# Normalizing k into zero-padded blocks, g into q, and w_out by column halves in a fused attention and feed-forward kernel

## The chip, the cores and the metric

The kernel runs on one core of a Trainium2 chip. A core has TensorE (PE, matrix products into PSUM; the profile lists its weight loads apart as PEld), VectorE (DVE), ScalarE (ACT), GpSimd (POOL) and SyncE (SP, which here only issues DMAs); 16 DMA engines move data between HBM and the on-chip memory SBUF, or inside SBUF. Each engine works its own instructions in order and waits on semaphores. The metric is the device time in microseconds (us) of one execution.

## What is computed

Attention over q, k, v of shape (8 batches, 12 heads, 448 positions, 64), with q and k RMS-normalized, followed by a feed-forward layer over 3584 rows of width 768 with 2048 hidden units and a hard-swish:

```python
def rmsnorm(x, g):
    rms = np.sqrt(np.mean(x * x, axis=-1, keepdims=True) + 1e-06)
    return x / rms * g
q_n, k_n = (rmsnorm(q, g_q), rmsnorm(k, g_k))
scores = (1.0 / np.sqrt(64)) * np.matmul(q_n, k_n.transpose(0, 1, 3, 2))
attn = softmax(scores)                  # exp(s - max) / sum
out = np.matmul(attn, v)                # heads side by side: x, 3584 x 768
h = x @ w_in
g = h * np.clip(h + 3.0, 0.0, 6.0) / 6.0
return (g @ w_out).astype(np.float32)
```

All inputs and the output are float32; the products run in bfloat16 and add up in float32.

## The kernel before

The work is cut into 48 pairs of heads (6 pairs a batch). A pair's 448 positions lie as three full blocks of 128 and a rest of 64; the rests of the two heads share one block. Two pairs make a group, and a group's q, k and v come by SP's DMAs into rings of three buffers (`q_st`, `k_st`, `v_st`; `load_q`, `load_k`, `load_v`, lines 248 to 275). For a pair p:

- `square` (line 306) on POOL, DVE or ACT, `stats_sum` (L315, a DVE reduce) and `stats_rstd` (L322, L325 on ACT) give 1/rms of every row. From group 8 on (`NFAST`) squares and normalizes are only on POOL.
- `normalize` (L330) writes k times 1/rms and q times 1/rms, as bfloat16, into `qk_r`, one instruction for k and one for q.
- For pairs 0 to 13 PE transposes the eight 128x128 blocks (`transposes`, L346), and `put_q` and `put_k` copy them from PSUM: q times g' = g_q g_k / 8 into `qT_r`, k into the zero-padded `kpad` (seven blocks; in blocks 0 to 2 only the first head's 64 rows are filled, in 4 to 6 only the second's).
- From pair 14 on (`TD`) one transposing DMA (`transposes_dma`, L352) moves the eight blocks from `qk_r` into `kqT_r`, a view of the weight staging buffers `w_st`; then `scale_k` (L361) multiplies the transposed k by g' into `kpad`, in two halves of 64 partitions, on DVE or POOL. q is read by PE as it was transposed.
- `score` (L375) makes seven products of 448 columns into two PSUM banks, `expo` (L381) takes their exponentials on ACT, `weigh` (L395, L401) multiplies by v with a column of ones, `divide` (L410, L411, DVE) divides, and x is transposed into `xT`, by PE and `put_x` for pairs 0 to 13 (L423, L434), by a DMA after that (L427).

The feed-forward of a batch needs the x of its six pairs: 16 `h` items (L438, six matmuls each), after each a `relu` (L444, ACT) and a `gate` (L449, DVE) that frees the PSUM bank and writes `gT`; then `y` items (L457, 16 matmuls of 384 columns for one block of 128 rows and one half of the columns), a copy to `y_r` (a view of `w_st`, three rows) and a store. `h` and `y` share three banks `m`, and the two score banks when attention is done. The weights come in 16 loads of 768 KB into the three buffers `w_st` (`load_w`, L288) and are cast to bfloat16 by `cast_w` (L278): eight of w_in by columns, eight of w_out by two row blocks each. Every `y` item waits for all eight of w_out.

The order is not written out by hand. `Plan` (line 41) holds every step with a key, dependencies, and for each engine that may do it an assumed duration; it walks through the time that these give, lets each engine take the known step with the smallest key, and choose among engines by when each would be done (POOL's durations count 0.4 of their length in this choice). On PE, `h` and `y` items fill in between attention's steps by a given share. What comes out is one fixed order of instructions on each engine and each DMA queue, so a changed duration in the plan changes orders everywhere.

Of the kernel before, what the change touches and what calls it, by code (L numbers as in the profile page):

```python
# [8 lines left out]
FP32 = mybir.dt.float32  # L9
BF16 = mybir.dt.bfloat16  # L10
# [35 lines left out]
class Plan:  # L46
# [5 lines left out]
    PRICE = {"POOL": 0.4}  # L52
# [104 lines left out]
def kernel(  # L157
# [29 lines left out]
    WR = 2  # L187
    NW = 3
    TD = 14
# [13 lines left out]
    gprime = const.tile([P, 1], FP32, name="gprime")  # L203
    eps_c = const.tile([P, 1], FP32, name="eps_c")
# [5 lines left out]
    kpad = ring(NK, [P, 7 * P], BF16, "kpad")  # L210
# [5 lines left out]
    qT_r = ring(NK, [P, S], BF16, "qT")  # L216
# [3 lines left out]
    t_r = ring(3, [P, S], FP32, "t_sb")  # L220
    w_st = ring(NW, [P, NKT * WC], FP32, "w_st")

    kqT_r = [w_st[i][:, 0:W4].bitcast(BF16).rearrange("p (a c) -> p a c", a=2) for i in range(NK)]
    y_r = [w_st[i][:, W4:W4 + DM] for i in range(3)]
# [55 lines left out]
    def load_w(n):  # L280
        if n < NWI:
            dst = w_st[n % NW][:].rearrange("p (kt f) -> p kt f", f=WC)
            src = moe_w_in[:, n * WC:(n + 1) * WC].rearrange("(kt p) f -> p kt f", p=P)
        else:
            c = (n - NWI) * WR * P
            dst = w_st[n % NW][:].rearrange("p (ft m) -> p ft m", m=DM)
            src = moe_w_out[c:c + WR * P, :].rearrange("(ft p) m -> p ft m", p=P)
        nc.sync.dma_start(out=dst, in_=src)  # L288

    def cast_w(eng, n):  # L290
        if n < NWI:
            out = w_in_sb[:, :, n * WC:(n + 1) * WC]
            in_ = w_st[n % NW][:].rearrange("p (kt f) -> p kt f", f=WC)
        else:
            c = (n - NWI) * WR
            out = w_out_sb[:, c:c + WR, :]
            in_ = w_st[n % NW][:].rearrange("p (ft m) -> p ft m", m=DM)
        copy(eng, out=out, in_=in_)
# [51 lines left out]

    def transposes_dma(p):
        nc.sync.dma_start_transpose(  # L352
            out=kqT_r[p % NK][:].rearrange("p a (t c) -> p (a t) c", t=4),
            in_=qk_r[p % NQ][:].rearrange("p a t h d -> p (a t h d)"),
        )

    def scale_k(eng, p, part):

        kp = kpad[p % NK]
        rows, c0 = ((lo, 0), (hi, NT * P))[part]  # L360
        eng.tensor_scalar_mul(kp[rows, c0:c0 + W4], kqT_r[p % NK][rows, 0, :], gprime[rows])  # L361

    def put_q(eng, p):
        if eng is nc.scalar:
            eng.activation(out=qT_r[p % NK][:], in_=t_ps[:, 1, 0:S], func=COPY, scale=gprime[:])
        else:
            eng.tensor_scalar_mul(qT_r[p % NK][:], t_ps[:, 1, 0:S], gprime[:])
# [6 lines left out]
    def score(p, i, n):  # L374
        nc.tensor.matmul(  # L375
            out=sc_r[n % 2][:, 0:S], lhsT=kpad[p % NK][:, i * P:(i + 1) * P],
            rhs=qT_r[p % NK][:] if p < TD else kqT_r[p % NK][:, 1, 0:S], start=True, stop=True,
        )
# [124 lines left out]

    def make_g():
# [57 lines left out]
    def y_item(b, t, part, place):  # L562
        n, c = YC, part * YC
        deps = [*w_ops[NWI:], *gates[b], *(gates[b - 1] if t == NT else [])]
# [4 lines left out]
        if part == 0:  # L569
            y_parts.append([])  # L570
        k = len(y_parts) - 1
# [4 lines left out]
        y_parts[k].append(it.out)  # L576
        if part == DM // YC - 1:
            stores.append(plan.dma((-1, 0), 1 if t < NT else 2, P * DM * 4,
                                   lambda: y_store(b, t, ys), y_parts[k]))

    def feed_forward(b):

        if b:
            ts = (NT, *range(NT)) if b % 2 == 0 else range(NT)
            ys = [(t, c) for t in ts for c in range(DM // YC)]
            for i, (t, c) in enumerate(ys):
# [5 lines left out]
    gate_ops, y_parts, y_rest = [], [], {}  # L592
    NWI = DFF // WC
    YC, YLAG = 384, 0.12
# [4 lines left out]
    for n in range(len(W_AFTER)):  # L599
        w_loads.append(plan.dma((GP * W_AFTER[n], 3 + n), 1, P * 1536 * 4, lambda n=n: load_w(n),  # L600
                                [at(w_ops, n - NW)], hold=True))
        w_ops.append(add((GP * W_AFTER[n], 9), [("DVE", 1350, lambda n=n: cast_w(V, n)),
# [14 lines left out]
    pad = by((0, 9), 1400, 1400, fill_e, [])  # L617
    squares = []
# [3 lines left out]
    for p in range(NPAIR):  # L622
        g = p // GP
        if p % GP == 0:
# [22 lines left out]
            for j, (p0, n) in enumerate(single):  # L647
                j = min(j, len(todo) - 1)
                for a in range(2):
                    m = len(squares)  # L650
                    s1 = add((p0 - 2, 2), [("POOL", 960 * n, lambda a=a, p0=p0, n=n, m=m: square(G, a, p0, n, m % 2)),
                                           ("DVE", 50 + 650 * n, lambda a=a, p0=p0, n=n, m=m: square(V, a, p0, n, m % 2)),
                                           ("ACT", 190 + 400 * n, lambda a=a, p0=p0, n=n, m=m: square(A_, a, p0, n, m % 2))][:3 if g < NFAST else 1],
# [14 lines left out]
        for a in range(2):  # L668
            nrm.append(add((p - 2, 4), [("POOL", 1070, lambda p=p, a=a: normalize(G, p, a)),
                                        ("DVE", 700, lambda p=p, a=a: normalize(V, p, a))][:2 if g < NFAST else 1],  # L670
                           [rstd_op[a, p], at(tr, p - NQ)]))
# [7 lines left out]
        if p >= TD:  # L679
            old = at(scs, 7 * (p - NK) + 6)  # L680
            tr.append(plan.dma_transpose((p - 1, 3), 4 * P * W4, lambda p=p: transposes_dma(p),
                               [nrm[2 * p], nrm[2 * p + 1], old, *w_ops[-NW:], at(pk, 2 * (p - NK)), at(pk, 2 * (p - NK) + 1)]))
            pq.append(tr[p])
            for part in range(2):
                pk.append(add((p - 1, 1 + part), [("DVE", 250, lambda p=p, part=part: scale_k(V, p, part)),
                                                  ("POOL", 500, lambda p=p, part=part: scale_k(G, p, part))],
                              [tr[p], mg, old]))
# [62 lines left out]
```

## Time and profile before

| | |
|---|---|
| median of 3 runs | 463.37 us (462.51 to 465.12) |
| the profiled execution | 462.64 us, span 460.8 us |
| busy: PE | 427.1 us, 93% |
| busy: DVE, ACT, POOL | 258.7, 292.2, 274.3 us |
| mean clock granted to PE | 0.981 |
| `scale_k` (L361) | POOL 34 of 1.586 us, DVE 34 of 1.108 us |
| `normalize` (L330) on POOL | 45 of k at 1.090 us, 44 of q at 1.092 us |
| transposing DMA of q and k (L352) | 34, median 3.1 us from issue to landing, longest 6.3 |
| moved by DMA | 70.60 MB, mean 153 GB/s |

A row of the groups names a line, an engine, what is written and read, and how often, then total and mean busy time. A row of stretches gives a start and an end, then for each engine the busy time in it. The chain of waits follows the work back from the end: at each step to what released it; its rows have a start, a length and what took it. In the table of 40 slices each digit is a busy share in tenths, and PEclk is the clock that PE was granted.

### The profile page before, as it was taken

To read this page: it belongs to the slowest core of one execution; us is meant where nothing else is said; L and a number is where in the kernel's file an instruction comes from. 1 tells how busy PE (TensorE), PEld (TensorE's weight loads), DVE (VectorE), ACT (ScalarE), POOL (GpSimd) and SP (SyncE) were. 2 spreads that over 40 slices of the span, in tenths; PEclk is the share of its full clock that TensorE was granted. 3 is DMA by queue.
4 is the path that set the end of the run, shared out by engine and by line. 5 is a ranking of instruction groups with operands and counts; after the bars stand their busy time and mean duration, and the time that the engine had idled before them with its cause. 6 is when DMAs were issued, how large, how long until landed. Compare 5 with 4: busy or idle time off the path is not lost.

```text
span 460.8 us, 9210 instructions
## 1 busy us (share of the span) xinstructions
PE 427.1 (93%) x3512; PEld 257.6 (56%) x3512; DVE 258.7 (56%) x420; ACT 292.2 (63%) x601; POOL 274.3 (60%) x249
## 2 busy tenths in 40 slices
PE   0787699699999989999999999999999999999996
PEld 0354466455566645665656656656666655555563
DVE  6689899855756656658565467576444243222300
ACT  3677878786476768768776677766766553333311
POOL 6799879984889779777897769696431000000000
PEclk9978999989999999999999999999999999999999
DMA  4899999992788897786696785934332220001021
GB/s 118 213 296 287 302 274 309 291 297 81 168 189 194 181 178 163 188 205 160 142 199 139 192 166 126 219 92 100 83 68 57 58 49 34 36 36 55 18 98 68
DMA packets 125804, 70.60 MB, mean 153 GB/s; under 512 B 77120, under 2 KB 120128, under 8 KB 125760
## 3 DMA queue, kind: packets, MB, share of 16 engines
q1 hardware_dynamic: 124928, 69.56, 60.0%
q8 instruction: 27, 0.44, 0.4%
q10 hardware_dynamic: 832, 0.46, 0.4%
q14 instruction: 17, 0.14, 0.1%
HBM read 45.61 MB, written 11.01 MB: 123 GB/s over the span
## 4 chain that ended last, share of the span: by engine, by line
PE 78%; DMA 6%; DVE 5%; SPq 5%; POOL 2%; issue 1%; ACT 1%; POOLq 0%; ACTq 0%
PE m L457 26%; PE m L438 25%; PE sc L375 10%; PE av L401 6%; PE sc L457 5%; DMA w_st<-qk 3%; PE sc L438 3%; PE av L395 2%; DMA w_st<-in_moe_w_in_dram 2%; DMA v_st<-in_v_dram 1%; SPq L275 1%; SPq L267 1%; DVE gT L449 1%; POOL qk L330 1%; DVE ssq L315 1%
## 5 line engine op out<-in xcount | busy, mean ns | idle before, releaser
L381 ACT ACTIVATE eT<-sc 128x448 bf16<-128x448 f32 x336 | 174.7, 543 | 66.5 <-PE sc L375 62.4
L438 PE MATMUL m<-xT,w_in_sb 128*128 128x448 bf16 x696 | 161.3, 352 | 4.0 <-DVE gT L449 3.6
L457 PE MATMUL m<-w_out_sb,gT 128*128 128x384 bf16 x768 | 150.1, 326 | 0.0
L457 PEld LDWEIGHTS <-gT 128*128 128x128 bf16 x896 | 87.0, 98 | 61.3
L438 PEld LDWEIGHTS <-w_in_sb 128*128 128x128 bf16 x768 | 74.4, 98 | 72.2 <-issue 6.1
L449 DVE SCALAR_TENSOR_TENSOR gT<-t_sb,m 128x448 bf16<-128x448 f32 x116 | 71.1, 619 | 60.8 <-ACT t_sb L444 59.7
L444 ACT ACTIVATE t_sb<-m,half_c 128x448 f32<-128x448 f32 x116 | 73.1, 633 | 24.0 <-PE m L438 21.9
L375 PE MATMUL sc<-w_st,kpad 128*128 128x448 bf16 x238 | 80.7, 352 | 0.5 <-ACT eT L381 0.5
L361 POOL TENSOR_SCALAR kpad<-w_st,gprime 64x512 bf16<-64x512 bf16 x34 | 53.9, 1586 | 18.8 <-DMA w_st<-qk 18.0
L315 DVE TENSOR_REDUCE ssq<-sq 128x16 f32<-128x1024 f32 (+1 forms) x56 | 58.7, 1060 | 4.4 <-POOL sq L312 2.8
L401 PE MATMUL av<-vaug,eT 128*128 128x65 bf16 x1152 | 56.7, 197 | 0.5 <-ACT eT L381 0.5
L401 PEld LDWEIGHTS <-eT 128*128 128x128 bf16 x1152 | 52.8, 101 | 5.2 <-issue 0.9
L330 POOL TENSOR_TENSOR qk<-k_st,rstd 128x512 bf16<-128x512 f32 x45 | 49.0, 1090 | 4.2 <-ACT rstd L325 3.4
L361 DVE TENSOR_SCALAR kpad<-w_st,gprime 64x512 bf16<-64x512 bf16 x34 | 37.7, 1108 | 20.6 <-DMA w_st<-qk 20.0
L330 POOL TENSOR_TENSOR qk<-q_st,rstd 128x512 bf16<-128x512 f32 x44 | 48.1, 1092 | 1.9 <-ACT rstd L325 1.7
L312 POOL TENSOR_TENSOR sq<-k_st 128x1024 f32<-128x1024 f32 (+1 forms) x24 | 41.9, 1747 | 11.2 <-DMA k_st<-in_k_dram 10.6
L312 POOL TENSOR_TENSOR sq<-q_st 128x1024 f32<-128x1024 f32 (+1 forms) x26 | 44.3, 1703 | 4.3 <-DMA q_st<-in_q_dram 2.6
L375 PEld LDWEIGHTS <-kpad 128*128 128x128 bf16 x336 | 31.2, 99 | 27.0 <-issue 6.2
L395 PE MATMUL av<-vaug,eT 128*128 128x130 bf16 x192 | 43.5, 227 | 0.0
L375 PE MATMUL sc<-qT,kpad 128*128 128x448 bf16 x98 | 35.4, 393 | 7.5 <-ACT eT L381 6.3
L278 POOL CAST vaug<-v_st 128x512 bf16<-128x512 f32 x34 | 21.0, 619 | 35.9 <-PE av L401 34.6
L278 ACT COPY w_st<-m 128x384 f32<-128x384 f32 x32 | 15.2, 476 | 30.3 <-PE m L457 28.0
(59 smaller groups left out, 254.4 us busy)
## 6 DMA issues: line engine op xcount, KB each, us to landing
out_dram<-w_st SPq DMA_DIRECT2D x24, 384.0 KB, 2.9
k_st<-in_k_dram SPq DMA_DIRECT2D x23, 384.0 KB, 4.1
q_st<-in_q_dram SPq DMA_DIRECT2D x23, 384.0 KB, 4.4
v_st<-in_v_dram SPq DMA_DIRECT2D x23, 384.0 KB, 4.5
w_st<-in_moe_w_in_dram SPq DMA_DIRECT2D x8, 768.0 KB, 7.0
w_st<-in_moe_w_out_dram SPq DMA_DIRECT2D x8, 768.0 KB, 6.0
out_dram<-w_st SPq DMA_DIRECT2D x8, 192.0 KB, 2.7
k_st<-in_k_dram SPq DMA_DIRECT2D x46, 32.0 KB, 3.6
```

The source lines that it names most:

```text
L312: eng.tensor_tensor(out=sq, in0=x, in1=x, op=A_MULT)
L315: nc.vector.tensor_reduce(out=ssq_r[(p // GP) % 2][:, a, p % GP:p % GP + n, :].rearrange("p r s -> p (r s)"), in_=sq_r[m][:, 0:n].rearrang ...
L330: eng.tensor_tensor(out=qk_r[p % NQ][:, a].rearrange("p t h d -> p h t d"), in0=raw(a, p, 1).rearrange("p r (h t) d -> p (r h) t d", h=2), ...
L361: eng.tensor_scalar_mul(kp[rows, c0:c0 + W4], kqT_r[p % NK][rows, 0, :], gprime[rows])
L375: nc.tensor.matmul(out=sc_r[n % 2][:, 0:S], lhsT=kpad[p % NK][:, i * P:(i + 1) * P], rhs=qT_r[p % NK][:] if p < TD else kqT_r[p % NK][:, 1 ...
L381: nc.scalar.activation(out=eT_r[n % NE][:, 0:S], in_=sc_r[n % 2][:, 0:S], func=EXP, bias=0.0, scale=1.0,)
L395: nc.tensor.matmul(out=av_ps[:, i, 0:2 * W], lhsT=e[3][:, cols], rhs=va[:, 3].rearrange("p h d -> p (h d)"), start=True, stop=False, skip_ ...
L401: nc.tensor.matmul(out=av_ps[:, i, h * W:(h + 1) * W], lhsT=e[4 * h + t][:, cols], rhs=va[:, t, h], start=False, stop=(t == NT - 1 and h = ...
L438: nc.tensor.matmul(out=m[:, 0:S], lhsT=w_in_sb[:, kt, f * P:(f + 1) * P], rhs=xT[:, kt, b % NX, x_slot(b)], start=(kt == 0), stop=(kt == N ...
L444: nc.scalar.activation(out=t[:], in_=m[:, 0:S], func=RELU, bias=half_c[:], scale=1.0 / 6.0,)
L449: nc.vector.scalar_tensor_tensor(out=gT[:, f, (b % 2) * S:(b % 2 + 1) * S], in0=t[:], scalar=1.0, in1=m[:, 0:S], op0=A_MIN, op1=A_MULT,)
L457: nc.tensor.matmul(out=m[:, 0:n], lhsT=gT[:, f, c0:c0 + P], rhs=w_out_sb[:, f, c:c + n], start=(f == 0), stop=(f == NFT - 1),)
```

## The change

- From pair 14 on `normalize_k` (POOL, one instruction a head) writes the normalized k straight into seven zero-padded blocks in `w_st` (`kq_st`; its zeros are set once by `clear_kq`, after the last weight casts), and `normalize_q` (DVE, eight instructions of 128x64) writes q times 1/rms times g' (`gq_b`, loaded by two broadcasting DMAs) behind them. One DMA transposes the eleven blocks into `kq_r`, of which `kpad` and `qT_r` are now views. `scale_k` is gone.
- w_out is loaded and cast by column halves, four row blocks at a time; a `y` item waits only for its half, and the `y` items of batch 0 are reordered to begin with the first half of two row blocks.
- `y_r` has its own two buffers.
- In the plan POOL's durations count 0.6 instead of 0.4, and the assumed durations of squares, normalizes and casts are others, by which three squares of groups 4 to 7 go to ACT, all weight casts to POOL, and the order of every engine shifts.

```diff
-    PRICE = {"POOL": 0.4}
+    PRICE = {"POOL": 0.6}
...
-    WR = 2
+    WR = 4
...
-    kpad = ring(NK, [P, 7 * P], BF16, "kpad")
+    kq_r = ring(NK, [P, 11 * P], BF16, "kq")
+    kpad = [x[:, 0:7 * P] for x in kq_r]
...
-    qT_r = ring(NK, [P, S], BF16, "qT")
+    qT_r = [x[:, 7 * P:7 * P + S] for x in kq_r]
...
+    y_r = ring(2, [P, DM], FP32, "y_sb")
...
-    kqT_r = [w_st[i][:, 0:W4].bitcast(BF16).rearrange("p (a c) -> p a c", a=2) for i in range(NK)]
-    y_r = [w_st[i][:, W4:W4 + DM] for i in range(3)]
+    KQ = 11 * P // 2
+    kq_st = [w_st[i][:, 0:KQ].bitcast(BF16) for i in range(NQ)]
...
-            c = (n - NWI) * WR
-            out = w_out_sb[:, c:c + WR, :]
+            half, r = divmod(n - NWI, NFT // WR)
+            out = w_out_sb[:, r * WR:(r + 1) * WR, half * YC:(half + 1) * YC]
...
+    def normalize_k(eng, p):
+        blocks = kq_st[p % NQ][:, 0:7 * P]
+        for h in range(2):
+            c0 = h * (NT * P)
+            eng.tensor_tensor(
+                out=blocks[:, c0:c0 + W4].rearrange("p (t c) -> p t c", t=4)[:, :, h * D:(h + 1) * D],
+                in0=raw(0, p, 1)[:, 0, 4 * h:4 * h + 4, :],
+                in1=rstd_r[(p // GP) % 2][:, 0, p % GP, 4 * h:4 * h + 4].unsqueeze(2)
+                .to_broadcast([P, 4, D]), op=A_MULT,
+            )
+
+    def normalize_q(p):
+        x = raw(1, p, 1)
+        out = kq_st[p % NQ][:, 7 * P:11 * P].rearrange("p (t h d) -> p t h d", t=4, h=2)
+        for h in range(2):
+            for t in range(4):
+                nc.vector.scalar_tensor_tensor(
+                    out=out[:, t, h, :], in0=x[:, 0, 4 * h + t, :],
+                    scalar=rstd_r[(p // GP) % 2][:, 1, p % GP, 4 * h + t:4 * h + t + 1],
+                    in1=gq_b[:], op0=A_MULT, op1=A_MULT,
+                )
...
-            out=kqT_r[p % NK][:].rearrange("p a (t c) -> p (a t) c", t=4),
-            in_=qk_r[p % NQ][:].rearrange("p a t h d -> p (a t h d)"),
-        )
-
-    def scale_k(eng, p, part):
-
-        kp = kpad[p % NK]
-        rows, c0 = ((lo, 0), (hi, NT * P))[part]
-        eng.tensor_scalar_mul(kp[rows, c0:c0 + W4], kqT_r[p % NK][rows, 0, :], gprime[rows])
+            out=kq_r[p % NK][:].rearrange("p (t c) -> p t c", c=P), in_=kq_st[p % NQ])
...
+    def clear_kq(eng, i):
+        blocks = kq_st[i][:, 0:7 * P].rearrange("p (t c) -> p t c", c=P)
+        eng.memset(blocks[:, 0:NT, D:P], 0.0)
+        eng.memset(blocks[:, NT + 1:7, 0:D], 0.0)
...
-        deps = [*w_ops[NWI:], *gates[b], *(gates[b - 1] if t == NT else [])]
+        deps = [*w_ops[NWI + part * NFT // WR:NWI + (part + 1) * NFT // WR], *gates[b], *(gates[b - 1] if t == NT else [])]
...
+            if b == 1:
+                ys = [(0, 0), (1, 0), (0, 1), (1, 1), (2, 0), (2, 1)]
...
-        w_ops.append(add((GP * W_AFTER[n], 9), [("DVE", 1350, lambda n=n: cast_w(V, n)),
+        w_ops.append(add((GP * W_AFTER[n], 9), [("DVE", 1500, lambda n=n: cast_w(V, n)),
...
+    ckq = [by((2 * TD, 0), 600, 350, lambda e, i=i: clear_kq(e, i), w_ops[-NW:]) for i in range(NQ)]
+    lgb = plan.dma((GP * 4, 0), 2, P * D * 8, load_gb)
+    mgb = add((GP * 5, 0), [("DVE", 300, make_gb)], [lgb])
...
-                                           ("DVE", 50 + 650 * n, lambda a=a, p0=p0, n=n, m=m: square(V, a, p0, n, m % 2)),
-                                           ("ACT", 190 + 400 * n, lambda a=a, p0=p0, n=n, m=m: square(A_, a, p0, n, m % 2))][:3 if g < NFAST else 1],
+                                           ("DVE", 1350 * n, lambda a=a, p0=p0, n=n, m=m: square(V, a, p0, n, m % 2)),
+                                           ("ACT", 170 + 445 * n, lambda a=a, p0=p0, n=n, m=m: square(A_, a, p0, n, m % 2))][:3 if g < NFAST else 1],
...
-        for a in range(2):
-            nrm.append(add((p - 2, 4), [("POOL", 1070, lambda p=p, a=a: normalize(G, p, a)),
-                                        ("DVE", 700, lambda p=p, a=a: normalize(V, p, a))][:2 if g < NFAST else 1],
-                           [rstd_op[a, p], at(tr, p - NQ)]))
+        if p < TD:
+            for a in range(2):
+                nrm.append(add((p - 2, 4), [("POOL", 1150, lambda p=p, a=a: normalize(G, p, a)),
+                                            ("DVE", 1250, lambda p=p, a=a: normalize(V, p, a))],
+                               [rstd_op[a, p], at(tr, p - NQ)]))
+        else:
+            nrm.append(add((p - 2, 4), [("POOL", 1250, lambda p=p: normalize_k(G, p))],
+                           [rstd_op[0, p], at(tr, p - NQ), ckq[p % NQ]]))
+            nrm.append(add((p - 2, 4), [("DVE", 1400, lambda p=p: normalize_q(p))],
+                           [rstd_op[1, p], at(tr, p - NQ), w_ops[-1], w_ops[-2], w_ops[-3], mgb]))
...
-            for part in range(2):
-                pk.append(add((p - 1, 1 + part), [("DVE", 250, lambda p=p, part=part: scale_k(V, p, part)),
-                                                  ("POOL", 500, lambda p=p, part=part: scale_k(G, p, part))],
-                              [tr[p], mg, old]))
+            pk += [tr[p], tr[p]]
```

## The prediction

> **What bounds the kernel now.** I read the page's first two parts, then the busy time of each engine by stretches that I cut where the PE row changes, then the chain of waits inside the two stretches that lose time, then the rows of the lines that the diff touches.
>
> The page:
>
> ```profile
> span 460.8 us, 9210 instructions
> PE 427.1 (93%) x3512; PEld 257.6 (56%) x3512; DVE 258.7 (56%) x420; ACT 292.2 (63%) x601; POOL 274.3 (60%) x249
> ...
> PEclk9978999989999999999999999999999999999999
> ```
>
> PE is busy for 93% of the span, so no other engine's share matters by itself; what can be won is PE's idle time and the slices in which its clock falls below 9 tenths.
>
> The busy time by stretches (start and end; length; PE, PEld, DVE, ACT, POOL; granted clock, DMA share, GB/s):
>
> ```profile
> 12.00:58.00 46.00, 34.84 (x327) 21.32 (x328) 36.77 (x65) 35.40 (x88) 40.88 (x37) 0.89 1.01 276
> 58.00:84.00 26.00, 25.95 (x256) 16.15 (x255) 24.01 (x45) 21.06 (x46) 22.83 (x19) 1.00 1.01 296
> 84.00:97.00 13.00, 8.39 (x92) 5.39 (x91) 9.05 (x15) 10.05 (x20) 12.94 (x11) 0.74 0.97 252
> 113.00:347.00 234.00, 230.80 (x1978) 140.76 (x1976) 143.19 (x203) 165.08 (x339) 176.75 (x144) 1.00 0.70 158
> 347.00:457.00 110.00, 110.00 (x728) 63.98 (x725) 28.22 (x48) 43.62 (x78) 1.56 (x1) 1.00 0.15 47
> ```
>
> From 58 us on PE is full but for two stretches. In 84 to 97 it is busy 8.39 of 13 us at clock 0.74, which is 6.2 us of work at full clock: 6.8 us lost. In 113 to 347 it idles 3.2 us. The rest of the loss is the start (12 us before the first scores) and 12 to 58, where the DMA engines are full (share 1.01) and the clock is 0.89.
>
> The chain of waits in the first of these stretches (start, us, what):
>
> ```profile
> 84.08 1.90 DVE qk L330
> ...
> 90.80 1.46 ACT w_out_sb L278
> 92.26 0.45 ACT eT L381
> 92.75 0.97 PE sc L375 x2
> ```
>
> Here PE has attention of pairs 10 to 12 alone, no feed-forward matmul of batch 0 being left, and it waits for one DVE normalize (1.90 us, against 0.69 when nothing holds it) and for a w_out cast that ACT does ahead of an exponential. In the second stretch:
>
> ```profile
> 162.28 6.28 DMA w_st<-qk
> 168.56 0.02 issue
> 168.58 0.35 DVE kpad L361
> 168.93 0.03 issue
> 168.96 0.63 DVE gT L449
> ...
> 298.47 3.24 DVE kpad L361
> ```
>
> DVE waits for a transposing DMA to land, because scale_k stands at the head of its queue, and the gate that frees a PSUM bank for PE stands behind it. Three such places (168, 270, 302) hold nearly all of the 3.2 us.
>
> **The change part by part.** The sum is made against this execution: 460.8 us of span and 1.8 around it, 462.64 us. The median of the runs shown, 463.37, lies 0.7 above.
>
> 1. scale_k goes (34 pairs, L361): 34 x 1.586 = 53.9 us of POOL and 34 x 1.108 = 37.7 us of DVE, none of it PE time. With it goes the only DVE instruction of the steady stage that waits for a DMA, so what it made late goes: the 3.2 us of idle PE. What is late next is a gate behind the new normalize_q (3). I take 2.2 us of gain; ends 0 and 3.2.
>
> 2. normalize_k (34 pairs, POOL, two instructions of 128x256 for one of 128x512 at 1.09): ends 1.09 (per column alone) and 1.3 (one POOL memset of little data, 0.1, as fixed cost, twice). 1.2. POOL also loses the q normalize (1.09 a pair). In 113 to 347 it falls from 176.75 to about 176.75 - 52.4 - 36.0 + 3.6 = 92 us of 234, 39%. Cover is not needed.
>
> 3. normalize_q (34 pairs, DVE, eight instructions of 128x64, two SBUF operands). No row shows one. The reduces of 128x1024 (1.212) and 128x512 (0.679) give 1.04 ns a column and 0.146 us fixed, so 64 columns are 0.213, eight are 1.7 us; two gates in a row started 0.53 apart at 0.61 each, so overlap could bring eight to 1.1. Above that comes waiting for POOL: the seven DVE normalizes of 128x512 took 1.27 on average, 0.58 over the free 0.69, while POOL was busy 88%. At 39% that is 0.26 an instruction: 0.3 if one of the eight is caught, 2.1 if all are. I take 1.7 + 1.0 = 2.7; ends 1.1 and 3.8. The transposing DMAs of before are issued from 113.4 to 346.9, 33 intervals of 7.08 us a pair. DVE has 143.2 / 33 = 4.3 us of work a pair, less 1.1, plus 2.7: 5.9 of 7.08, so it is covered by DVE's idle time. A gate behind it can be 2 to 3 us late; I leave 1.0 us of the idle time of (1) standing for that. Without the cover see rival B.
>
> The Trainium skill (SBUF — State Buffer, Who interferes with whom) says that a DVE instruction with two SBUF inputs and a GpSimd instruction that reads SBUF lock each other out whole. The trace agrees: at 51.05 a DVE normalize took 1.53 us, ending 0.54 after the POOL normalize that held it. That rule speaks against moving q from POOL to DVE in eight pieces; were each piece caught by a whole 1.09 us instruction the sum would gain nothing and rival B would hold, with POOL's lower load as its limit.
>
> 4. The transposing DMA takes 11 blocks for 8. Four blocks land in a median 3.0 us and eight in 3.1, so about 3.2; the longest of eight took 6.3. It is issued some 15 us before the pair's first score (162.3 against 177.2 for pair 22), and the scale that followed is gone: nothing on the path, ends 0 and, if a landing of 6.3 met a late issue, 1 us. On the engines: 256-byte packets took 22 ns (113 to 119 us), 34 x 3 x 128 x 22 ns / 16 = 18 us in 234, share 0.70 to 0.78.
>
> 5. w_out by halves and y of batch 0 reordered. In the new order PE starts y of batch 0 inside the weigh of pair 11, after t13, where before it had only h of batch 1, after x11. Between the last h of batch 0 and that point stand 10 scores, one weigh, two transposes of qk and one of xn (4.1 us of PE); before there were 14 scores, two weighs and more. ACT starts exponentials 0.49 apart, so 4.9 us is the floor, and DVE's chain from weigh 10 to t13 (0.9 divide, 1.3 puts, 0.4 x, 1.2 reduce, 0.4 put) with the hops some 5 to 7. So 1 to 3 us lost for 6.8; I take 3.0, a gain of 3.8, ends 0 and 5.8. It needs the four casts of the first half of w_out. All 16 weight casts are now on POOL; adding the mean durations of its rows along POOL's new order, the last cast of the first half stands behind 75 us of POOL work and the last of all behind 86, where before the last one on POOL stood behind 96 and ended at 113. POOL was 12 us behind its own work by 80 us, so 88 and 99; PE should come to y at about 89 to 90. The ACT cast at 90.80 is gone with it.
>
> The w_out packets are 1,536 bytes for 3,072. Packets of 1,024 took 55 ns and of 3,072 141, so 76: 1.5 us more of all engines, under the full PE of 58 to 84. Nothing; without that cover 1.5.
>
> 6. Squares early: three of 128x1024 go from POOL (1.89) to ACT, at about twice the 0.62 of 128x512. ACT loses two casts of 1.46. Nothing on PE in 12 to 58, where the DMA queue order of the first seven groups is nearly unchanged; the first transposes now wait for POOL's k behind a v cast: 0.3 us of loss, ends -2 and +2.
>
> 7. SP: two loads of gq_b, gk_b (under 1 us each) pass ahead of a k load at full PE: nothing, at most 1. The transpose of pair 15 stands ahead of that of 14, then a store that waits for the second half of y, then the k and q of group 10, which was loaded at 90 and will be at about 115. Pair 20 is scored near 160: 30 us of slack over a 15 us chain. Six POOL memsets (0.2 to 0.4) and normalize_q of 14 wait for the last cast near 99; pair 14 is scored near 118, and its chain (memsets, three normalizes, DMA 3.2) ends near 109. In the DVE queue the gates of h of batch 1 stand behind that normalize_q; it is reached near 105. Nothing, or rival C.
>
> 8. y has two buffers for three: a row takes 32 x 0.163 = 5.2 us, a store 2.9 plus issue. Nothing; 1 us if stores queue on SP.
>
> Sum: -2.2 - 3.8 + 0.3 = -5.7, a span of 455.1 and 456.9 us; I give 456.8.
>
> **Rivals.** A: the head gives nothing, because PE reaches y before the first-half casts (five casts later than 90 us would do) or waits for the same DVE chain. For: POOL is 12.94 of 13 us busy there. Against: 10 us less work ahead of the casts. Only (1) stays: 460.5.
>
> B, slower: DVE becomes the bound of the steady stage, gates are late, PE waits for banks. It decides from 7.08 - 3.2 = 3.9 us of normalize_q a pair. Each piece caught for 0.31 would make 4.2, 0.34 x 34 = 12 us lost, and (1) lost too: 470. For: POOL and DVE alternated at 51 us, and eight pieces give eight chances. Against: POOL is at 39%.
>
> C: the last casts come 6 us late or more (weight loads in a full DMA queue), normalize_q of pair 14 holds DVE, and the gates of batch 1 wait: 5 us back, 462.
>
> D: 12 to 58 shortens as well, by 4 us of its 11 idle ones, since POOL passes its early work sooner: 452.8. For: POOL is busy 40.88 of 46. Against: DMA share 1.01.
>
> **The numbers.** Forecast 0.56, A 0.13, B 0.15, C 0.08, D 0.08. A measurement can tell about 0.5% (2.3 us) from no change: under 461.1 is faster, over 465.7 slower. Faster: forecast, D and two thirds of A, 0.73; same: the rest of A and C, 0.12; slower: B, 0.15. Range 450 to 467: D and the gain ends of (1) and (5) below, C and a mild B above; what is left out is most of B and little else. The forecast alone has 453 to 460.5.
>
> **What would show it.** Right: no idle time of DVE behind the transposing DMA; PE busy over 232 of 234 us in the steady stage, POOL near 39%; y of batch 0 starting near 90 us instead of 117, clock near 1 from 84 to 97. Wrong: eight pieces over 3.9 us a pair, gates that wait for DVE and PE that waits for gates; PE waiting for a w_out cast near 90; scores waiting for the transposing DMA.

## The result, and the profile after

The changed kernel takes 476.64 us (median of 4 runs, 473.59 to 478.0) against 463.22 for the kernel before: a ratio of 1.027, 95% interval 1.022 to 1.033. It is slower by 13 us, where a gain of some 6 us was forecast, and it lies above the forecast range of 450 to 467 us.

The first two parts of the page of the changed kernel (the profiled execution took 473.59 us, the least of the four and 3 us under their median):

```profile
span 471.8 us, 9390 instructions
PE 427.8 (91%) x3512; PEld 256.7 (54%) x3512; DVE 306.7 (65%) x659; ACT 291.3 (62%) x602; POOL 194.8 (41%) x221
...
PEclk9979999999999999999999979999999999999999
```

PE has the same work and 11 us more of span. DVE went from 258.7 to 306.7 us, POOL from 274.3 to 194.8. The same stretches as before (start and end; length; PE, PEld, DVE, ACT, POOL; granted clock, DMA share, GB/s):

```profile
12.00:58.00 46.00, 32.17 (x322) 19.65 (x323) 34.69 (x65) 35.71 (x87) 37.76 (x35) 0.93 0.94 260
...
84.00:97.00 13.00, 11.00 (x120) 7.03 (x118) 9.11 (x17) 8.48 (x20) 10.91 (x7) 1.00 1.10 322
...
113.00:347.00 234.00, 221.20 (x1852) 133.07 (x1850) 190.19 (x419) 155.33 (x322) 103.48 (x113) 0.99 0.79 170
347.00:457.00 110.00, 110.00 (x767) 64.34 (x766) 33.01 (x61) 51.18 (x93) 1.53 (x3) 1.00 0.20 54
```

The head came as forecast: 84 to 97 loses 2.0 us at full clock, where it lost 6.8. The steady stage, 113 to 347, idles 12.8 us of PE where it idled 3.2. What PE waited for in that stage (engine, line, releaser: us in total, times, longest):

```profile
PE m L460 <- DVE gT L471: 7.8, 7, 4.0
PE t_ps L445 <- DVE xT L456: 2.2, 1, 2.2
PE sc L397 <- ACT eT L403: 2.1, 2, 1.5
```

Banks that a gate has not freed. No score waits for the transposing DMA. The chain of waits at two of these places:

```profile
213.68 5.98 DMA kq<-w_st
219.66 0.03 issue
219.69 2.48 DVE w_st L375 x8
222.17 0.54 DVE gT L471
222.71 0.04 issue
222.75 0.73 PE m L460 x3
...
274.32 4.02 DVE w_st L375 x8
278.34 0.54 DVE gT L471
278.88 0.04 issue
278.92 1.65 PE m L460 x4
```

`normalize_q` (L375) stands at the head of DVE's queue with a gate behind it. It waits itself for a transposing DMA, the one of three pairs before that still reads its staging buffer; then its eight pieces take 2.5 to 4 us. The line's own rows:

```profile
L375 DVE SCALAR_TENSOR_TENSOR w_st<-q_st,rstd,gq_b x272: 267/273/1948, 108.7 to 348.1; 128x64 bf16<-128x64 f32 x136
...
  DMA kq<-w_st: 16.1, 15
```

A piece takes 273 ns in the median and up to 1948; DVE stood idle for the DMA 16.1 us in 15 places.

Three things could make these gates late: the wait, the length, or the order in which the plan put the steps. Two measures of them are used below. A gate's lateness is its start less the end of the relu that it needs (0.03 us at best), for the gates of 113 to 347 us. PE's loss at x us of work is the start of a matmul less the full-clock time of all matmuls ahead of it in PE's order (189 ns for 448 columns, 162.5 for 384, 31 to 57 for the small ones); all of them are 410 us.

| PE's loss, us | at 40 of work | at 66 | end | from 66 to the end |
|---|---|---|---|---|
| before | 33.8 | 41.7 | 46.7 | 5.0 |
| changed | 34.8 | 38.2 | 57.4 | 19.2 |

So the head (up to 66) won 3.5 us in this profile, and the steady stage lost 14.2 more than before. Step (6) at the end shows that other profiles of this head lost up to 5 us more by 40 us of work, so the 3.5 us are not a safe gain; the loss after 66 us is free of that.

### The profile page after: what moved, and what is told of

Same layout as the page of the kernel before. It is cut to its first block, busy times and chain, and to the rows that moved or that the text cites. A ratio compares the mean times of both kernels' runs of the same rounds, so it can differ in the third digit from the quotient of the medians.

```text
span 471.8 us, 9390 instructions
## 1 busy us (share of the span) xinstructions
PE 427.8 (91%) x3512; PEld 256.7 (54%) x3512; DVE 306.7 (65%) x659; ACT 291.3 (62%) x602; POOL 194.8 (41%) x221
## 4 chain that ended last, share of the span: by engine, by line
PE 70%; DMA 11%; DVE 7%; SPq 5%; ACT 2%; issue 2%; POOL 1%; POOLq 0%; ACTq 0%
PE m L479 24%; PE m L460 22%; PE sc L397 9%; PE av L423 6%; DMA kq<-w_st 6%; PE sc L479 4%; DVE w_st L375 4%; DMA v_st<-in_v_dram 3%; PE sc L460 2%; DMA k_st<-in_k_dram 2%; DVE ssq L321 2%; PE av L417 2%; SPq L280 1%; SPq L272 1%; POOL sq L318 1%
## 5 line engine op out<-in xcount | busy, mean ns | idle before, releaser
L460 PE MATMUL m<-xT,w_in_sb 128*128 128x448 bf16 x708 | 167.3, 355 | 8.8 <-DVE gT L471 7.8
L397 PE MATMUL sc<-kq 128*128 128x448 bf16 x336 | 116.3, 361 | 11.7 <-ACT eT L403 10.3
L375 DVE SCALAR_TENSOR_TENSOR w_st<-q_st,rstd,gq_b 128x64 bf16<-128x64 f32 x272 | 96.5, 422 | 16.2 <-DMA kq<-w_st 16.1
L363 POOL TENSOR_TENSOR w_st<-k_st,rstd 128x256 bf16<-128x256 f32 x68 | 40.6, 619 | 31.0 <-DMA kq<-w_st 25.7
L318 POOL TENSOR_TENSOR sq<-k_st 128x1024 f32<-128x1024 f32 (+1 forms) x23 | 39.2, 1706 | 22.9 <-DMA k_st<-in_k_dram 12.3
L397 PEld LDWEIGHTS <-kq 128*128 128x128 bf16 x336 | 31.4, 99 | 28.8 <-issue 7.9
L283 ACT COPY y_sb<-m 128x384 f32<-128x384 f32 x36 | 17.3, 479 | 37.0 <-PE m L479 37.0
L433 DVE TENSOR_TENSOR xn<-av,rden 128x512 bf16<-128x512 f32 x48 | 33.2, 691 | 1.7
L432 DVE RECIPROCAL rden<-av 128x8 f32<-128x8 f32 x48 | 9.8, 203 | 28.0 <-PE av L423 27.5
L328 ACT ACTIVATE lnv<-ssq,eps_c 128x32 f32<-128x32 f32 (+1 forms) x36 | 11.1, 309 | 19.8 <-DVE ssq L321 19.6
```

What stands on the lines that cost most here:

```text
L318: eng.tensor_tensor(out=sq, in0=x, in1=x, op=A_MULT)
L363: eng.tensor_tensor(out=blocks[:, c0:c0 + W4].rearrange("p (t c) -> p t c", t=4)[:, :, h * D:(h + 1) * D], in0=raw(0, p, 1)[:, 0, 4 * h:4 ...
L375: nc.vector.scalar_tensor_tensor(out=out[:, t, h, :], in0=x[:, 0, 4 * h + t, :], scalar=rstd_r[(p // GP) % 2][:, 1, p % GP, 4 * h + t:4 * ...
L397: nc.tensor.matmul(out=sc_r[n % 2][:, 0:S], lhsT=kpad[p % NK][:, i * P:(i + 1) * P], rhs=qT_r[p % NK], start=True, stop=True,)
L460: nc.tensor.matmul(out=m[:, 0:S], lhsT=w_in_sb[:, kt, f * P:(f + 1) * P], rhs=xT[:, kt, b % NX, x_slot(b)], start=(kt == 0), stop=(kt == N ...
```

## The experiments

### Wait, length or order

Six staging buffers take the wait away:

```diff
-    kq_st = [w_st[i][:, 0:KQ].bitcast(BF16) for i in range(NQ)]
+    NB = 2 * NQ
+    kq_st = [w_st[i % NQ][:, i // NQ * KQ:(i // NQ + 1) * KQ].bitcast(BF16) for i in range(NB)]
```

> The changed kernel with six staging buffers in place of three for the eleven blocks (six more POOL memsets; the order of all other instructions is that of the changed kernel). normalize_k and normalize_q then need no longer wait until the transposing DMA of three pairs before has read their buffer. Theory W (the wait): the lost time comes from DVE standing in its queue for that DMA (15 waits, 16.1 us) with gates behind it. Then these waits go to near zero, PE's idle time in 113 to 347 us falls from 12.8 to 4-6 us, and the kernel takes 466 to 470 us. Theory S (the size): the eight pieces at 2.84 us a pair, and the lock against POOL, make the gates late by themselves; then the waits go as well but the time stays at 474 to 477. Theory O (the order): what costs is the new order of loads and steps around 97 to 140 us; then the time stays at 474 to 477 too, with PE's gaps between 120 and 140 us unchanged.

Measured: 473.14 us, ratio 1.023 (1.019 to 1.027). Its group row and its chain at the place shown above:

```profile
L376 DVE SCALAR_TENSOR_TENSOR w_st<-q_st,rstd,gq_b 128x64 bf16<-128x64 f32 x272 | 94.6, 417 | 0.0
```

```profile
274.78 5.51 DVE w_st L376 x8
280.30 0.54 DVE gT L472
```

The wait is gone (idle before it 0.0 us), and the gates are hardly sooner (1.25 us late in the mean for 1.39). PE still loses 14.3 us after 66 us of work, for 19.2: of the 14.2 us that the steady stage lost, some 4.9 go with the wait.

The length, with the wait left in place:

```diff
-        for h in range(2):
-            for t in range(4):
-                nc.vector.scalar_tensor_tensor(
...
+        nc.vector.tensor_tensor(
+            out=out.rearrange("p t h d -> p h t d"),
...
```

> The changed kernel with normalize_q as one DVE instruction of 128x512 for eight of 128x64; it leaves out the factor g' for pairs 14 to 47, so the scores are not the reference's. Same order of instructions, same wait for the transposing DMA. normalize_q falls from 2.84 to about 0.9 us a pair, 66 us of DVE in all. Theory S: most of the loss goes, 464 to 468 us. Theory W: the waits of DVE for the DMA stay at 13 to 18 us, and PE gains only by each gate coming up to 1.9 us sooner: 470 to 474. Theory O: 474 to 477.

Measured: 462.40 us, ratio 0.998 (0.995 to 1.001). Its group row:

```profile
L373 DVE TENSOR_TENSOR w_st<-q_st,rstd 128x512 bf16<-128x512 f32 x34 | 29.4, 864 | 23.3 <-DMA kq<-w_st 22.7
```

DVE waits for the DMA even longer, 22.7 us, and it costs nothing: PE loses 3.1 us after 66 us of work, less than the kernel before. The kernel before had such a wait too, in 113 to 347 us (us in total, times, longest), beside a loss of 5.0 us:

```profile
DVE kpad L361 <- DMA w_st<-qk: 20.0, 12, 3.6
```

The order of PE's matmuls is the same from first to last in this run, in the one with six buffers and in the changed kernel. The loss is the length's, more than theory S asked for. The late k load of group 10 that the chain of the changed kernel shows near 122 us is in this order too, and PE loses 0.2 us between 80 and 120 us of work (5.3 in the changed kernel): alone it costs nothing.

The old path of k and q under the changed head:

```diff
-        if p < TD:
-            for a in range(2):
-                nrm.append(add((p - 2, 4), [("POOL", 1150, lambda p=p, a=a: normalize(G, p, a)),
...
-            nrm.append(add((p - 2, 4), [("DVE", 1400, lambda p=p: normalize_q(p))],
...
+            for part in range(2):
+                pk.append(add((p - 1, 1 + part), [("DVE", 250, lambda p=p, part=part: scale_k(V, p, part)),
+                                                  ("POOL", 500, lambda p=p, part=part: scale_k(G, p, part))],
+                              [tr[p], mg, old]))
```

> The changed kernel with the old path of k and q from pair 14 on (both normalized on POOL, eight blocks transposed, scale_k), but w_out by halves, y of batch 0 reordered, y rows in buffers of their own and the changed prices of the plan kept. Theories W and S: all that the change lost lies in the new path, so the loss goes and the 3.7 us of the head stay: 458 to 461 us against 463 before. Theory O: the loss lies in what the plan makes of the changed prices and the later loads; then it takes 466 to 472.

Six buffers with the plan told of them:

```diff
-                           [rstd_op[1, p], at(tr, p - NQ), w_ops[-1], w_ops[-2], w_ops[-3], mgb]))
+                           [rstd_op[1, p], at(tr, p - (NB if p >= TD + NB else NQ)), w_ops[-1], w_ops[-2], w_ops[-3], mgb]))
```

> The kernel with six staging buffers, and the plan told so: it may put normalize_k and normalize_q of a pair ahead of the transposing DMA of three pairs before, which changes the order of steps. Theory W: as with six buffers alone, 464 to 470 us. Theory S: 474 to 477. Theory O: the order is another, so the time can go either way, with gaps of PE in 113 to 140 us that differ from those of the changed kernel.

Measured: 465.33 us, 1.005 (1.003 to 1.007), and 487.66 us, 1.053 (1.050 to 1.056). Both miss the ranges: 465.33 lies between theory S's 458 to 461 and theory O's 466 to 472, and 487.66 is above all figures given; only theory O had left the second open. With the old path PE loses 8.2 us after 66 us of work, 5.0 of them between 120 and 150; with the plan told of six buffers it loses 30.5, although DVE waits for the DMA 1.4 us in all. So the order matters by itself, a reading that the next runs return to.

### What makes it long: POOL in between

A stretch of the changed kernel's timeline (start, us, engine, line; the eight pieces are one row):

```profile
291.08 1.89 POOL L318 TENSOR_TENSOR sq<-k_st 128x1024 f32<-128x1024 f32 x1
...
292.02 4.81 DVE L375 SCALAR_TENSOR_TENSOR w_st<-q_st,rstd,gq_b 128x64 bf16<-128x64 f32 x8 [0.15 <-DMA kq<-w_st]
...
292.93 1.18 POOL L363 TENSOR_TENSOR w_st<-k_st,rstd 128x256 bf16<-128x256 f32 x2
...
294.47 1.89 POOL L318 TENSOR_TENSOR sq<-q_st 128x1024 f32<-128x1024 f32 x1 [0.36 <-DMA q_st<-in_q_dram]
```

The eight pieces here took 1028, 647, 648, 272, 272, 1936, 271 and 271 ns: one that meets a `normalize_k` half (0.61) lasts 0.65, one that meets a square (1.89) lasts 1.94. Pairs that met no POOL instruction took 1.65 us from first start to last end; 9 of 34 took over 3.5.

Eight pieces that read one tensor:

```diff
-                nc.vector.scalar_tensor_tensor(
-                    out=out[:, t, h, :], in0=x[:, 0, 4 * h + t, :],
+                nc.vector.tensor_scalar_mul(
+                    out[:, t, h, :], x[:, 0, 4 * h + t, :],
...
```

> The changed kernel with the eight pieces of normalize_q as multiplications by 1/rms alone (one tensor from SBUF and a scalar per partition, no second tensor); it leaves out g' for pairs 14 to 47, so the scores are not the reference's. Theory L (the lock: a piece with two tensors from SBUF that meets a POOL instruction lasts as long as that one, 0.65 us beside 0.61 and 1.93 beside 1.89, against 0.27 alone, and with eight pieces POOL gets in between again and again): a piece with one tensor is not held, every pair takes about 1.65 us from start to end, and the kernel takes 461 to 466 us. Theory N (the number: eight instructions are too much work for DVE, however long each is): busy DVE falls only as far as the pieces get shorter, and the kernel takes 468 to 473. If one tensor from SBUF is held just as two are, pieces of 0.65 and 1.93 us stay and it takes 472 to 477.

Measured: 472.09 us, 1.022 (1.017 to 1.027). The row:

```profile
L375 DVE TENSOR_SCALAR w_st<-q_st,rstd x272: 241/244/1939, 110.3 to 344.4; 128x64 bf16<-128x64 f32 x136
```

A piece alone is 244 ns; those that met POOL still took 0.65 and 1.93, so one tensor is held here as two are. This tells nothing between L and N. A long DVE step that POOL does not hold does:

```diff
+        nc.vector.tensor_reduce(
+            out=spare[:], in_=w_in_sb[:, 0, 0:1792].rearrange("p (s d) -> p s d", d=D),
+            axis=mybir.AxisListType.X, op=A_ADD,
+        )
```

> The kernel with normalize_q as one DVE instruction (without g' for pairs 14 to 47, so the scores are not the reference's), and behind each of them one DVE reduce of 128x1792 of weights whose result nobody reads, some 1.9 us that POOL has not been seen to hold. DVE does about 2.8 us a pair there, as much as with the eight pieces, but evenly. Theory N (how much DVE does decides): the loss comes back, 471 to 477 us. Theory L (the holds by POOL decide: 4 to 5.5 us in a row where two squares get in between, 1.65 where none does): the gates are late by 2.8 us at most, and it takes 463 to 468.

Measured: 473.21 us, 1.022 (1.015 to 1.029). The rows of the reduce (by line) and of the one instruction (by group) are of two views:

```profile
L380 DVE TENSOR_REDUCE spare<-w_in_sb x34: 2005/2007/2014, 112.8 to 345.0; 128x28 f32<-128x1792 bf16 x34
```

```profile
L374 DVE TENSOR_TENSOR w_st<-q_st,rstd 128x512 bf16<-128x512 f32 x34 | 30.0, 882 | 9.8 <-DMA kq<-w_st 9.5
```

Every reduce took 2.01 us whatever POOL did, 2.89 a pair in all, and the loss is back: 14.6 us after 66 us of work, in the same order of PE's matmuls. Theory L falls: the length alone, without peaks, is enough. That the peaks add some of the changed kernel's 19.2 is not ruled out. The hold by POOL matters in that it makes 1.65 us into 2.84.

Two complete kernels with a shorter step, one with two whole instructions on DVE, one with g' multiplied on POOL:

```diff
+        flat = kq_st[p % NQ][:, 7 * P:11 * P].rearrange("p (s d) -> p s d", d=D)
+        nc.vector.tensor_tensor(
+            out=flat, in0=flat, in1=gq_h[:].unsqueeze(1).to_broadcast([P, 8, D]), op=A_MULT,
+        )
```

> The changed kernel, complete, with normalize_q as two whole DVE instructions: 128x512 by 1/rms (0.86 us where it was measured alone), then 128x512 in bfloat16 by g' in place. Theory L: two chances to meet POOL for eight, about 1.5 to 1.9 us a pair, so most of the loss goes: 462 to 467 us. Theory N: the same, since two instructions are fewer. The theory of the wait alone: 472 to 476.

```diff
+    def scale_q(p):
+        x = raw(1, p, 1).rearrange("p r s d -> p (r s) d")
+        nc.gpsimd.tensor_tensor(
+            out=x, in0=x, in1=gq_b[:].unsqueeze(1).to_broadcast([P, 8, D]), op=A_MULT,
+        )
```

> The changed kernel, complete, with g' multiplied into raw q on POOL (34 more instructions of 128x512, some 1.1 us each) and normalize_q as one DVE instruction of 128x512 by 1/rms. DVE is as light as with one instruction (0.86 us a pair); POOL goes from 44% to some 60% in 113 to 347 us. Theory L: DVE meets POOL more often but only once a pair: 461 to 467 us. If POOL's extra step comes too late for normalize_q, DVE waits for POOL in its queue: 466 to 472. The added step also moves the order of the others.

Measured: 464.23 us, 1.000 (0.997 to 1.004), and 463.29 us, 0.998 (0.994 to 1.002). Both give back what the change lost; neither wins.

### Why 2.8 us a pair is too much for a DVE that is 81% busy

The plan puts `normalize_q` at 1400 ns. One number changed:

```diff
-            nrm.append(add((p - 2, 4), [("DVE", 1400, lambda p=p: normalize_q(p))],
+            nrm.append(add((p - 2, 4), [("DVE", 2850, lambda p=p: normalize_q(p))],
```

> The changed kernel with one number of the plan changed: normalize_q is taken to last 2850 ns (what it took) in place of 1400, so the fixed order of all engines from pair 14 on is made for its real length. Theory Q (the order was made for a normalize_q of half its length, so it stands ahead of gates that then come late): PE's loss after 66 us of work done falls from 19.2 us to 8 to 12, and the kernel takes 464 to 469 us. Theory R (DVE has no room: with 5.8 us of work in some 7.1 us a pair, in one queue with waits, gates are late in any order): 473 to 478.

Measured: 464.50 us, 1.006 (1.003 to 1.008): 10 to 12 us for one number in the plan (by the ratios and by the medians). Stretch and group row:

```profile
113.00:347.00 234.00, 229.77 (x1964) 139.36 (x1963) 182.51 (x441) 168.33 (x346) 100.93 (x110) 1.00 0.79 176
```

```profile
L375 DVE SCALAR_TENSOR_TENSOR w_st<-q_st,rstd,gq_b 128x64 bf16<-128x64 f32 x272 | 80.5, 364 | 4.6 <-DMA kq<-w_st 4.6
```

DVE is still 78% busy there, and PE idles 4.2 us for 12.8. The wait for the DMA fell from 16.1 to 4.6 us without a buffer more, and with the order otherwise arranged fewer pieces meet POOL (2.37 us a pair for 2.84). PE's loss after 66 us of work, 6.7 us, is even under the 8 to 12 of theory Q. The shorter pieces are not the reason for most of it: at 2.50 us a pair, in the order made for 1.4, PE lost 15.6.

With six buffers on top, and six buffers under the two whole instructions (the edits shown above, in one kernel each):

> The same number in the plan, and the six staging buffers too, so that normalize_q does not wait for the transposing DMA either. Theory Q: PE's loss after 66 us of work falls from 14.3 us (six buffers alone) to 5 to 8, 462 to 466 us. Theory R: 470 to 474, as with six buffers alone.

> The complete kernel with normalize_q as two whole DVE instructions, and six staging buffers: its 23.5 us of DVE waits for the transposing DMA go. With the eight pieces six buffers won 4.9 us of PE's loss in the steady stage; here that loss is 5.8 us and 3.1 with one instruction, so 0 to 3 us can be won: 461 to 464 us.

Measured: 464.40 us, 1.003 (1.001 to 1.005), and 461.75 us, 0.998 (0.995 to 1.001). With the price right the buffers win nothing more. The runs side by side:

| kernel | `normalize_q`, us a pair | planned | gates late, mean us | over 2 us late | PE's loss after 66 us of work | time |
|---|---|---|---|---|---|---|
| before | | | 0.58 | 8 of 67 | 5.0 | 463 |
| one instruction, no g' | 0.86 | 1.4 | 0.33 | 2 of 71 | 3.1 | 462.4 |
| two whole instructions | 1.52 | 1.4 | 0.67 | 6 of 72 | 5.8 | 464.2 |
| two whole, six buffers | 1.85 | 1.4 | 0.48 | 2 of 72 | 4.5 | 461.8 |
| eight, one tensor | 2.50 | 1.4 | 1.18 | 13 of 68 | 15.6 | 472.1 |
| changed | 2.84 | 1.4 | 1.39 | 17 of 66 | 19.2 | 476.6 |
| six buffers | 2.78 | 1.4 | 1.25 | 18 of 68 | 14.3 | 473.1 |
| six buffers, plan told | 2.80 | 1.4 | 1.53 | 22 of 63 | 30.5 | 487.7 |
| one and a reduce | 2.89 | 1.4 | 1.36 | 14 of 68 | 14.6 | 473.2 |
| changed, price 2.85 | 2.37 | 2.85 | 0.70 | 10 of 71 | 6.7 | 464.5 |
| the same, six buffers | 2.34 | 2.85 | 0.67 | 9 of 71 | 6.4 | 464.4 |

Near its planned length the step costs at most a microsecond of PE against before; 1 us and more beyond it, 9 us and more. With the true length in the plan, the same eight pieces cost 2 us against before. The length is not all: at the same planned and nearly the same real length, the order made for six buffers loses twice what the other does. Why that order is so much worse was not tried, and the true length was tried in only two orders, this one and that of the last section.

### The head

The plan's other prices as they were before, under the complete kernels with g' on POOL and with two whole instructions:

```diff
-    PRICE = {"POOL": 0.6}
+    PRICE = {"POOL": 0.4}
...
-                                           ("DVE", 1350 * n, lambda a=a, p0=p0, n=n, m=m: square(V, a, p0, n, m % 2)),
+                                           ("DVE", 50 + 650 * n, lambda a=a, p0=p0, n=n, m=m: square(V, a, p0, n, m % 2)),
...
```

> The complete kernel with g' multiplied on POOL and one DVE instruction for normalize_q, and now with the plan's prices for squares, normalizes of pairs 0 to 13, weight casts and POOL as they were before the change; w_out by halves stays. Theory P (the prices moved early work to POOL and cost 2 to 6 us of PE's time by 40 us of work done): PE's loss by then falls to that of the kernel before, 33.8 us, and with 4 us won from the halves of w_out it takes 458 to 461 us. If the early order does not matter: 462 to 465, as with the new prices.

> The complete kernel with normalize_q as two whole DVE instructions, and the plan's prices as they were before the change. Theory P: 2 to 4 us less than with the new prices, 460 to 462 us. If the early order does not matter: 463 to 465.

Measured: 466.27 us, 1.009 (1.006 to 1.012), and 464.98 us, 1.007 (1.004 to 1.010). Theory P falls: PE's loss at 40 us of work is 36.9 and 36.4, no lower than the 34.8 to 39.7 with the new prices, and the times are no shorter.

The kernel before with w_out by halves alone (the lines of the change that bear on `WR`, `YC`, the loads, casts and dependencies of y, and `y_r`; `kpad` and `qT_r` become views of one ring, as in the change):

```diff
-    WR = 2
+    WR = 4
...
+    y_r = ring(2, [P, DM], FP32, "y_sb")
...
+            if b == 1:
+                ys = [(0, 0), (1, 0), (0, 1), (1, 1), (2, 0), (2, 1)]
```

> The kernel before with the halves of w_out, the order of y of batch 0 and two y rows of their own alone: old prices, old path of k and q. If the halves are worth what PE's loss between 40 and 66 us of work done says (3.6 us for 7.9) and the early order is as before: 458 to 461 us. If the gain is lost to the larger number of smaller packets, or the plan's order changes with it: 462 to 465.

And with one thing more, the casts of w_out kept on POOL:

```diff
-                                               ("ACT", 1450, lambda n=n: cast_w(A_, n))], [w_loads[n]]))
+                                               ("ACT", 1450, lambda n=n: cast_w(A_, n))][1 if n >= NWI else 0:2 if n >= NWI else 3], [w_loads[n]]))
```

> The kernel before with halves of w_out, its y order and y rows, and the eight casts of w_out on POOL alone. In the kernel with the halves alone, PE's two gaps near 88 and 92 us (2.24 and 2.17 us) stood behind a DVE normalize held by POOL and behind a w_out cast on ACT ahead of an exponential. If the cast is what kept the halves from paying, the second gap goes: 460 to 462.5 us. If y of batch 0 waits for casts on POOL instead: 463 to 467.

Measured: 465.13 us, 1.007 (1.004 to 1.009), and 459.43 us, 0.993 (0.991 to 0.995). The chain of waits with the halves alone:

```profile
84.16 1.90 DVE qk L333
...
90.85 1.46 ACT w_out_sb L280
92.31 0.45 ACT eT L385
92.77 0.04 issue
92.81 0.97 PE sc L379 x2
```

and with the casts off ACT:

```profile
83.30 1.90 DVE qk L333
...
89.41 0.63 ACT kq L369
90.04 0.44 ACT eT L385
90.48 0.04 issue
90.53 0.97 PE sc L379 x2
```

The halves alone leave both gaps of before in place, since y of batch 0 starts only behind them; without the cast one of the two goes, and PE's loss at 66 us of work falls from 41.6 to 39.1. The loss after 66 falls more, from 6.9 to 1.9; why was not tried. The profiled execution with the casts off ACT took 456.98 us, 2.5 us under the median, so these steps may be somewhat too large.

### The two parts together, mended

To the last kernel comes the new path of k and q, with six buffers, a planned length near the real one (1700 ns for 1.84 us) and the loads of gq_b and gk_b later:

```diff
-    lgb = plan.dma((GP * 4, 0), 2, P * D * 8, load_gb)
-    mgb = add((GP * 5, 0), [("DVE", 300, make_gb)], [lgb])
+    lgb = plan.dma((GP * 7, 0), 2, P * D * 8, load_gb)
+    mgb = add((GP * 7 - 1, 0), [("DVE", 300, make_gb)], [lgb])
...
-            nrm.append(add((p - 2, 4), [("DVE", 1400, lambda p=p: normalize_q(p))],
+            nrm.append(add((p - 2, 4), [("DVE", 1700, lambda p=p: normalize_q(p))],
```

> The new path of k and q on top of the best head found: old prices, halves of w_out with their casts kept off ACT, the two loads of gq_b and gk_b three groups later (which gives PE the same order as that kernel up to 52 us of work), normalize_q as two whole instructions planned at 1700 ns, six staging buffers. The kernel with the old path and the same head takes 459.4 us and loses 1.9 us of PE after 66 us of work, which leaves the new path at most that to win. If the new path is by now as good as the old one: 458 to 461 us; if it costs what two whole instructions with six buffers lost (4.5 us after 66 us of work): 461 to 464.

> The same with normalize_q left as the change has it, in eight pieces, planned at 2850 ns. With the new prices this way lost 6.9 us after 66 us of work, 5.0 more than the old path loses with this head, of which the length of the pieces itself takes a part: 461 to 465 us, so better than the kernel with the price alone (464.5) by what the head gives, and worse than the old path (459.4).

Measured: 458.44 us, 0.990 (0.987 to 0.994), with two whole instructions and six buffers; 459.69 us, 0.993 (0.990 to 0.996), with the eight pieces and their true price (also on six buffers). The stretches of the first:

```profile
84.00:97.00 13.00, 11.09 (x121) 6.87 (x120) 9.48 (x19) 10.35 (x22) 13.00 (x10) 1.00 0.94 301
...
113.00:347.00 234.00, 231.63 (x1958) 140.64 (x1957) 167.85 (x243) 165.68 (x337) 119.47 (x123) 1.00 0.80 172
```

Both are faster than the kernel before, by 1.0 and 0.7%, and than the changed one. Against the same head with the old path of k and q (459.43) the new path wins 1 us or nothing: the two intervals overlap, and these runs do not tell them apart. Of the eight pieces I had expected 461 to 465 us.

## Why the prediction was wrong, by its steps

The step that failed is (3): "covered by DVE's idle time", with 1.0 us of idle PE left standing for late gates. The length was nearly right (2.84 for 2.7, within 1.1 to 3.8) and so was DVE's load (81% measured; 5.9 of 7.08 us, 83%, forecast). But room in the mean is no cover in a queue whose order was made for half that length: gates came 1.39 us late for 0.58, and PE lost 14 us more after 66 us of work, not 1. The number was in the diff, 1400, beside an estimate of 2.7, and the two were never compared. Rival B had the mechanism, with the wrong point from which it decides: 3.9 us a pair, worked out from room alone. In the order made for 1.4 it set in between 1.5 and 2.5.

(1) With `scale_k` "the only DVE instruction of the steady stage that waits for a DMA" was to go, and the late gates with it. But `normalize_q` waits for one too, 16.1 us, because its staging ring has three buffers. Nor does such a wait cost much by itself: with the old path, the halves and the casts off ACT, DVE waits 26.0 us for this DMA in 20 places, and PE loses 1.9 us after 66 us of work. That the old path leaves some 2 us to win is borne out by one profile only (3.1 us with one short instruction, for 5.0); that kernel's time is the same as before.

(2) `normalize_k` took 2 x 0.619 = 1.24 us (forecast 1.2), POOL 44% in the steady stage (39%).

(3), the hold by POOL: 1.2 us a pair above the free 1.65; forecast 1.0. The rule of the Trainium skill that stood beside it (SBUF — State Buffer, Who interferes with whom) is borne out piece by piece: 0.65 us beside POOL's 0.61, 1.93 beside 1.89.

(4) The transposing DMA landed in 4.2 us (median; 3.5 to 6.0), forecast 3.2; no score waited for it, as forecast. DMA share 0.79 for 0.78. What waited was the next user of its source buffer, which the step did not look at.

(5) 84 to 97 lost 2.0 us for 6.8 (forecast 3.0), y of batch 0 began at 92.2 (90). The reason given was half of it: by halves alone y begins at 95.3, behind both gaps, and nothing is won; keeping the casts off ACT closes one of them. The size was near: between 40 and 66 us of work the changed kernel and the ten others with its head and its path lost 3.4 to 3.8 us, for 7.9 before, a gain of 4.1 to 4.5 for the 3.8 forecast.

(6) 0.3 us of loss, ends -2 and +2, was too small. At 40 us of work the changed kernel and the ten made from it with the same prices and the new path lost 34.8 to 39.7 us, mean 37.4; the kernel before and the three with the old path 33.0 to 34.0. That is 3.5 us and more in the mean, and in most runs it ate the gain of (5). The prices of the plan do not look like the cause: with the new prices and the old path the loss is 34.0, with the old prices and the new path 36.4 and 36.9. With the loads of gq_b and gk_b three groups later PE's order is that of the old path up to 52 us of work, and the loss 35.1 and 35.7. These are single profiles, which differ by up to 4 us in the same order, so which step costs the 3.5 us is open.

(7) and (8) cost nothing that shows between 66 us of work and the end, as forecast: the run with one instruction has the same loads and buffers and loses 3.1 us there. Whether the two loads of gq_b and gk_b have a part in (6) is open.

## What to carry to other kernels

When an order is fixed by assumed durations, compare every assumed duration in a change with your own estimate, and treat a step that outlasts its planned length as work in the way of what is queued behind it, however idle the engine is in the mean. A step cut into small DVE instructions gives POOL a chance to hold it at each cut; two whole instructions of the same work were 1.3 us a pair shorter here, and 0.9 with six buffers. When two parts of a change pull in opposite directions, run each on the other's base: here the head was worth 3 us only with its casts off ACT (part of that came after the head, for a reason not found), and the path cost 13 us only with a wrong price.

## What the runs showed of the hardware

- A DVE piece of 128x64 that multiplies one SBUF tensor by a scalar per partition (244 ns alone) is held by POOL as long as one with two tensors (273): 0.65 beside 0.61, 1.93 beside 1.89. Theory L had taken it to be free. The Trainium skill (SBUF — State Buffer, Who interferes with whom) names `tensor_scalar`, under conditions on its operands, among the forms that can contend with GpSimd, and reduces among those that on this chip never do; the runs agree with both, 34 reduces having taken 2005 to 2014 ns beside a busy POOL.
- The hold goes both ways: a half of `normalize_k` on POOL took 0.62 us beside the eight pieces, 0.82 beside one DVE instruction of 128x512 and 0.88 beside two (means of all 68). In the run with one instruction the 26 halves that met no `normalize_q` took 0.61 us each, and the 42 that met one 0.95 in the mean.
- Three kernels with the same order of instructions up to 100 us (the changed one, six buffers, one instruction) lost 34.8, 38.9 and 36.4 us at 40 us of work. So single profiles of this head do not tell apart kernels that differ by less than 4 us there.
